# Loads of q and k for five of eight batches as casting transfers issued by GpSimd, and their turns split into 64 columns

## The chip, the cores and the metric

The kernel runs on one core of a Trainium2 chip. The metric is the device time of one launch in microseconds, lower is better. Matrix products and transposes run on TensorE (PE; PEld is its weight load), elementwise work on VectorE (DVE), ScalarE (ACT) and GpSimd (POOL). SyncE (SP) computes nothing here: it issues transfers between the chip's memory (HBM) and the on-chip buffer (SBUF). Products land in eight banks of a separate memory (PSUM).

## The reference

An attention in two parts, followed by a layer that mixes over tokens and channels. Cut to what is computed, with B = 8 batches, H = 8 heads, S = 576 positions, D = 64:

```python
q_d, k_d, v_d = means of q, k, v over groups of 4 positions          # 144 positions
out_d   = softmax(q_d k_d^T / 8) v_d, each row repeated 4 times
out_loc = softmax over |i - j| < 4 of (q k^T / 8), times v
x = (out_up + out_loc) as [B, S, H * D]                              # 576 x 512
theta = x @ w_theta
y = w_tok_r @ (x * cos(theta)) + w_tok_i @ (x * sin(theta))          # over positions
u = x + y
out = u + max(u @ w_ch, 0)
```

Inputs and output are float32; the kernel works in bfloat16 between.

## The kernel before

The kernel is a set of generators, one for each step of a batch: `load`, `cast`, `turns`, `turns_out`, `key_sums`, `query_sums`, the pooled attention, the local attention (`scores`, `masks`, `outputs`), then `phases`, `waves`, `products`, `mix`, `channels`, `store`. The string `ORDER`, written out by hand, says which step runs next, one letter each ("L" a load, "C" a cast, "A" a turn), with steps of several batches interleaved. `pin()` ties every instruction to the one before it on its engine, so each engine works in exactly this order, and an instruction that waits holds everything behind it on its engine. Waits between engines follow from the data. The string `BANKS` gives each product its bank, and `ENGINES` gives each copy its engine: the string `C` has one letter per cast (p GpSimd, a ScalarE, v VectorE).

How q and k of one batch come in:

- `load` (L213) issues, from SP's queue, eight transfers of 288 KB, two heads each (`k0` to `k3`, `q0` to `q3`, L223), into float32 staging tiles `st`, of which 15 rotate. A row holds 9 positions of 64 numbers (`WR` = 9), so a partition gets 2304 bytes in one piece. Five chunks of v follow, two transfers each (L220).
- `cast` (L226) copies each staging tile to bfloat16: `k_tm` and `q_tm`, two buffers each, laid out as [pair of transfers, position in the row, transfer, 64], so that the 128 columns of one position (two transfers of 64) lie next to each other. All copies share line 127.
- `turns` (L294) transposes on TensorE: for each of four groups (k of transfers 0 and 1, q of 0 and 1, k of 2 and 3, q of 2 and 3) nine transposes of 128 x 128 (L300) into two banks. Each needs both casts of its group.
- `turns_out` copies the result to `kT` and `qT`; from there go the sums over four positions (`key_sums` on VectorE, L317; `query_sums` on GpSimd, L334 and L335) and the local scores (L468).

GpSimd also does some of the casts of v and of the weights, the multiplies of `pooled_v_last` (L363, tile `vd`) and some of the copies `ut`. `pooled_v` (L348, L350) multiplies v on TensorE by 32-column matrices; L350 needs the fifth chunk of v. `weight_turns` (L276) transposes the token weights; its ninth group is made of transposes of 64 columns, two of them side by side onto the lower and the upper 64 partitions of a bank. The longest work on TensorE is `mix` (L654): nine products of 288 columns for each of 8 pieces of a batch. For batches 6 and 7, `x_turns_by_queue` borrows a `k_tm` buffer for transposes done by transfers (L628).

Of the kernel before, what the change touches and what calls it, by code (L numbers as in the profile page):

```python
# [9 lines left out]
BF16 = mybir.dt.bfloat16  # L10
# [4 lines left out]
P = 128  # L15
# [3 lines left out]
D = 64  # L19
# [15 lines left out]
WR = 9  # L35
# [2 lines left out]
HALF = 64  # L38

BY_QUEUE = [6, 7]  # L40

OC = 96

# [2 lines left out]
def kernel(  # L46
# [11 lines left out]
    nc = tc.nc  # L58
# [29 lines left out]
        C=(  # L88
            "vapaaaaavpvvappppppapppvpapppppppppppppvapvpappvappapppppppavpvapappaapppaaaaapppppaaaapapppappp"
            "appaavaa"  # L90
        ),
        a="avaavaaaavaaaaaaaaaaaaaaaaaaaaaa",
        c="aapapppappppppppappp",
        f="ppvpapap",
        q="vaaavvva",
# [8 lines left out]
    def rot(tag, shape, dt, n):  # L104
        k = turn[tag] = turn.get(tag, -1) + 1
        if (tag, k % n) not in made:
            made[tag, k % n] = const.tile(shape, dt, name=f"{tag}_{k % n}")
        return made[tag, k % n]
# [9 lines left out]
    def two(dt=FP32):  # L118
        i = int(next(banks)) // 2
        ap = space[:, 2 * i:2 * i + 2, :]  # L120
        return ap if dt == FP32 else ap.bitcast(dt)

    copies = dict(v=nc.vector.tensor_copy, a=nc.scalar.copy, p=nc.gpsimd.tensor_copy)
    engines = {s: iter(e) for s, e in ENGINES.items()}

    def copy(step, **operands):
        copies[next(engines[step])](**operands)  # L127
# [3 lines left out]
    def tile_of(name, shape, dt=BF16):  # L131
        return const.tile(shape, dt, name=name)

    ident = tile_of("ident", [P, P])
# [70 lines left out]
    staged, inputs = {}, {}  # L205

    def stage(key):
        t = staged[key] = rot("st", [P, S], FP32, 15)
        return t

    ITEMS = ["k0", "k1", "q0", "q1", "k2", "k3", "q2", "q3", "v0", "v1", "v2", "v3", "v4"]

    def load(b):  # L213
        for it in ITEMS:
            c = int(it[1])
            if it[0] == "v":
                t = stage((b, it))[:, 0:DM].rearrange("p (h d) -> p h d", d=D)
                for g in range(2):
                    lo = W0[2 * c + g]
                    nc.sync.dma_start(out=t[W * g:W * g + W], in_=v[b, :, lo:lo + W, :].rearrange("h p d -> p h d"))  # L220
            else:
                src = k if it[0] == "k" else q
                nc.sync.dma_start(out=stage((b, it)), in_=src[b, 2 * c:2 * c + 2].rearrange("h (p r) d -> (h p) (r d)", r=WR))  # L223
            yield

    def cast(b):  # L226
        k_tm = rot("k_tm", [P, 2, WR, 2, D], BF16, 2)
        q_tm = rot("q_tm", [P, 2, WR, 2, D], BF16, 2)
        v_w = v_ws[b % 2]
        inputs[b] = (q_tm, k_tm, v_w)  # L230
        for it in ITEMS:
            c = int(it[1])
            if it[0] == "v":
                copy("C", out=v_w[:, c, :, 0:D], in_=staged.pop((b, it))[:, 0:DM].rearrange("p (h d) -> p h d", d=D))
            else:
                dst = k_tm if it[0] == "k" else q_tm
                copy("C", out=dst[:, c // 2, :, c % 2, :], in_=staged.pop((b, it)).rearrange("p (r d) -> p r d", d=D))
            yield


# [53 lines left out]
    def turns(b):  # L294
        q_tm, k_tm, v_w = inputs[b]
        parts[b] = (rot("qT", [P, 4, S], BF16, 2), kTs[b % 2], rot("qdT", [P, 4, SD], BF16, 2), kds[b % 2])
        for i, what in TURNS:
            ps = held["turn", b, i, what] = two(BF16).rearrange("p k e -> p (k e)")
            for r in range(WR):
                nc.tensor.transpose(out=ps[:, P * r:P * r + P], in_=(k_tm if what == "k" else q_tm)[:, i, r, :, :], identity=ident)  # L300
            yield

    def turns_out(b):
# [318 lines left out]
    xms = {}  # L622

    def x_turns_by_queue(b):
        spare = rot("k_tm", [P, 2, WR, 2, D], BF16, 2).rearrange("p i r c d -> p (i r c d)")
        xm = xms[b] = spare[:, 0:4 * DM].rearrange("p (c n) -> p c n", c=4)
        for dc in range(4):
            nc.sync.dma_start_transpose(out=xm[:, :, P * dc:P * dc + P], in_=xTs[b][:, dc, 0:512])  # L628
            yield

    def products(b):
        for c in range(4):
            x = xms[b][:, c, :] if b in BY_QUEUE else held.pop(("xt", b, c))
            nc.vector.tensor_tensor(  # L634
# [108 lines left out]
    def each(steps, n=B):  # L743
        for b in n if isinstance(n, list) else range(n):
            yield from steps(b)

    sequences = {
        "k": constants(), "1": table(AF.Sin), "2": table(AF.Exp),
        "L": each(load), "C": each(cast), "l": weight_loads(), "c": weight_casts(), "V": weight_turns(), "v": weight_turns_out(),
        "A": each(turns), "a": each(turns_out), "d": each(key_sums), "e": each(query_sums),  # L750
        "U": each(pooled_v), "u": each(pooled_v_out), "x": each(pooled_v_last),
        "P": each(pooled_scores), "p": each(pooled_exp), "N": each(pooled_out), "n": each(pooled_norm),
# [3 lines left out]
        "T": each(transposes), "t": each(transposes_out),  # L756
        "H": each(phases), "h": each(waves), "G": each(tail_phases), "g": each(tail_waves), "Z": each(tail_product), "z": each(tail_z),
        "X": each(x_turns, [b for b in range(B) if b not in BY_QUEUE]), "M": each(x_turns_by_queue, BY_QUEUE), "y": each(products),
        "J": each(mix), "j": each(mix_out),
        "R": each(residual), "f": each(tail_gather), "F": each(tail_residual, B // 2),  # L760
# [40 lines left out]
```

## Time and profile before

| | |
|---|---|
| time, median of 2 runs | 244.81 us (244.55 to 245.08) |
| profiled execution | 245.89 us, of which the span from the first to the last instruction is 244.2 us |
| TensorE busy | 214.8 us (88% of the span) |
| VectorE, ScalarE, GpSimd busy | 191.3, 164.9, 95.0 us |
| transfers | 50.91 MB, mean 208 GB/s; SP's queue 91.7% of 16 engines' span |
| `st` from k and q | 64 transfers of 288 KB, median 4.8 and 5.3 us from issue to landing |
| casts of `q_tm` and `k_tm` | 64, about 0.67 us each: 43 on GpSimd, 18 on ScalarE, 3 on VectorE |

Busy times are of one profiled execution, so sums from it are set against its own span; the median is of other runs. A busy TensorE includes the modelled ends of pipelined products: a product counts 286 ns (L654) while the next one starts 122 ns later. The share of the transfers is the time that packets took on 16 engines; it can pass 1 in a stretch, since packets overlap. In the views, a line of the timeline has the start, the length, the engine, the line of the kernel, the tiles (out<-in), the form and the count, and in brackets the idle time before it with what ended it.

### The profile page before, as it was taken

Reading aid. Unit: us, or ns where it says so; the run is one execution under the profiler, and the core shown is the slowest. Engines: PE = TensorE matmul, PEld = TensorE weight load, DVE = VectorE, ACT = ScalarE, POOL = GpSimd, SP = SyncE. Lnnn points to the kernel's source line nnn. Section 1 sums busy time; section 2 is a strip of 40 time slices with the busy share of each in tenths; the row PEclk is TensorE's granted clock in tenths of the full one; section 3 lists DMA queues with packets and bytes.
Section 4 is the critical chain, followed back from the end, with each engine's and each line's share of the span. In section 5 each row is a group of like instructions: output and inputs, shape, how many; then the busy total and the mean of one; then the engine's idle time right before and its main releaser. Section 6 shows DMA issues by size and latency. Waiting matters only on the chain.

```text
span 244.2 us, 8224 instructions
## 1 busy us (share of the span) xinstructions
PE 214.8 (88%) x3344; PEld 151.8 (62%) x3344; DVE 191.3 (78%) x393; ACT 164.9 (68%) x240; POOL 95.0 (39%) x170
## 2 busy tenths in 40 slices
PE   1466586998999999799999999999999999999990
PEld 1354453776678685487775786676676765667740
DVE  3596977797789879779799988897798978585453
ACT  3786497699799899798899859866677653420000
POOL 1785585776574594272056115923021000000000
PEclk9999997799999999999999999999999999999997
DMA  6999989989999999999899989997531586966577
GB/s 203 280 211 295 278 179 241 312 206 189 263 299 227 280 273 149 194 267 268 194 244 271 146 240 262 283 217 161 99 124 51 136 124 159 173 170 154 59 230 229
DMA packets 87671, 50.91 MB, mean 208 GB/s; under 512 B 72529, under 2 KB 72785, under 8 KB 87633
## 3 DMA queue, kind: packets, MB, share of 16 engines
q1 hardware_dynamic: 87632, 50.38, 91.7%
q8 instruction: 26, 0.43, 0.8%
q14 instruction: 13, 0.10, 0.2%
HBM read 34.11 MB, written 9.44 MB: 178 GB/s over the span
## 4 chain that ended last, share of the span: by engine, by line
PE 47%; DMA 22%; DVE 13%; SPq 7%; POOL 3%; issue 3%; ACT 3%; DVEq 0%; ACTq 0%; POOLq 0%
PE space L654 18%; DMA st<-in_v_dram 10%; PE space L567 7%; PE space L693 6%; DMA st<-in_q_dram 5%; SPq L220 4%; PE space L300 3%; DVE osb L706 2%; PE space L500 2%; DMA st<-in_moe_w_tok_i_dram 2%; PE space L540 2%; SPq L255 2%; DVE z L634 2%; DMA ur<-uT 1%; SPq L628 1%
## 5 line engine op out<-in xcount | busy, mean ns | idle before, releaser
L654 PE MATMUL space<-WT,z 128*128 128x288 bf16 x576 | 79.4, 286 | 0.8 <-DVE uT L663 0.4
L654 PEld LDWEIGHTS <-z 128*128 128x128 bf16 x576 | 54.0, 98 | 17.1 <-issue 1.3
L663 DVE TENSOR_TENSOR uT<-space,xT 128x288 bf16<-128x288 f32 x64 | 28.1, 449 | 11.5 <-PE space L654 9.6
L567 PE MATMUL space<-wth,xT 128*128 128x512 bf16 x128 | 33.8, 389 | 0.1
L693 PE MATMUL space<-wch,uT 128*128 128x512 bf16 (+1 forms) x132 | 31.9, 373 | 0.0
L706 DVE SCALAR_TENSOR_TENSOR osb<-space,ur 128x512 f32<-128x512 f32 (+1 forms) x33 | 21.7, 666 | 10.1 <-DMA ur<-uT 6.4
L574 ACT ACTIVATE cs<-space,pihc 128x512 bf16<-128x512 f32 x32 | 22.2, 693 | 7.9 <-issue 3.9
L520 DVE TENSOR_TENSOR tmp<-space,rl 128x512 bf16<-128x512 f32 x40 | 26.7, 679 | 0.5
L552 DVE TENSOR_TENSOR xT<-space,xdT 128x464 bf16<-128x464 f32 (+1 forms) x40 | 24.7, 627 | 1.7 <-PE space L540 1.4
L317 DVE TENSOR_REDUCE kd<-kT 128x290 bf16<-128x1160 bf16 x16 | 21.6, 1353 | 2.8 <-ACT kT L127 2.8
L480 ACT ACTIVATE pm<-space 128x1024 bf16<-128x1024 f32 (+1 forms) x24 | 20.6, 882 | 3.6 <-PE space L468 3.4
L334 POOL TENSOR_TENSOR two<-qT 128x576 f32<-128x576 bf16 x14 | 16.2, 1157 | 15.6 <-ACT qT L127 8.6
L127 POOL CAST q_tm<-st 128x576 bf16<-128x576 f32 x23 | 15.6, 685 | 15.6 <-DMA st<-in_q_dram 15.2
L127 POOL CAST k_tm<-st 128x576 bf16<-128x576 f32 x20 | 13.9, 700 | 18.8 <-DMA st<-in_k_dram 17.7
L127 POOL COPY ut<-uT 128x256 bf16<-128x256 bf16 x5 | 2.3, 451 | 44.5 <-DVE uT L663 44.5
L127 POOL CAST v_w<-st 128x512 bf16<-128x512 f32 x16 | 10.0, 634 | 23.9 <-DMA st<-in_v_dram 21.8
L575 ACT ACTIVATE cs<-space 128x512 bf16<-128x512 f32 x32 | 19.1, 598 | 0.0
L127 ACT COPY qT<-space 128x1152 bf16<-128x1152 bf16 x14 | 15.7, 1120 | 4.8 <-PE space L300 4.7
L693 PEld LDWEIGHTS <-uT 128*128 128x128 bf16 x132 | 12.1, 98 | 10.6 <-issue 0.3
L127 ACT COPY kT<-space 128x1152 bf16<-128x1152 bf16 x15 | 17.0, 1132 | 2.3 <-PE space L300 1.9
L567 PEld LDWEIGHTS <-xT 128*128 128x128 bf16 x128 | 11.5, 100 | 10.2 <-issue 0.8
L300 PE MATMUL space<-ident,k_tm 128*128 128x128 bf16 x144 | 12.1, 236 | 6.4 <-ACT k_tm L127 6.1
(95 smaller groups left out, 397.1 us busy)
## 6 DMA issues: line engine op xcount, KB each, us to landing
st<-in_v_dram SPq DMA_DIRECT2D x80, 128.0 KB, 5.1
st<-in_k_dram SPq DMA_DIRECT2D x32, 288.0 KB, 4.8
st<-in_q_dram SPq DMA_DIRECT2D x32, 288.0 KB, 5.3
out_dram<-osb SPq DMA_DIRECT2D x31, 256.0 KB, 3.3
st<-in_moe_w_tok_r_dram SPq DMA_DIRECT2D x6, 216.0 KB, 5.1
st<-in_moe_w_tok_i_dram SPq DMA_DIRECT2D x6, 216.0 KB, 4.8
out_dram<-osb SPq DMA_DIRECT2D x10, 128.0 KB, 2.5
st<-in_moe_w_theta_dram SPq DMA_DIRECT2D x4, 256.0 KB, 6.3
```

The source lines that it names most:

```text
L127: copies[next(engines[step])](**operands)
L300: nc.tensor.transpose(out=ps[:, P * r:P * r + P], in_=(k_tm if what == "k" else q_tm)[:, i, r, :, :], identity=ident)
L317: nc.vector.tensor_reduce(out=kd[:, hs, :, 0:PG].rearrange("p e g m -> p (e g) m"), axis=AX.X, op=ALU.add, in_=kT[:, hs, :].rearrange("p e ...
L480: nc.scalar.activation(out=pm.rearrange("p e c j w -> p e (c j w)"), in_=held.pop(("S", b, u))[:, :, 0:4 * W * n], func=AF.Exp, scale=SCL)
L520: nc.vector.tensor_tensor(out=tmp.rearrange("p g (j d) -> p g j d", d=D), in0=held.pop(("loc", b, c))[:, :, :, 0:D], in1=rls.pop((b, c)).u ...
L552: nc.vector.tensor_tensor(out=xT[:, :, CH * c:CH * c + cnt].rearrange("p e (m j) -> p e m j", j=4), in0=held.pop(("xT", b, c))[:, :, 0:cnt ...
L567: nc.tensor.matmul(out=th, lhsT=xT[:, dc, P * c:P * c + P], rhs=wth[:, dc, :], start=(dc == 0), stop=(dc == 3))
L574: nc.scalar.activation(out=cs[:, 0, :], in_=th, func=AF.Sin, bias=pihc, scale=1.0)
L654: nc.tensor.matmul(out=ps, lhsT=z[:, j, P * dc:P * dc + P], rhs=WT[:, j, 288 * hf:288 * hf + 288], start=(j == 0), stop=(j == 8))
L663: nc.vector.tensor_tensor(out=uT[:, dc, cols], in0=held.pop(("u", b, dc, hf)), in1=xT[:, dc, cols], op=ALU.add)
L693: nc.tensor.matmul(out=ps, lhsT=uT[:, dc, P * c:P * c + P], rhs=wch[:, dc, cols], start=(dc == 0), stop=(dc == 3))
L706: nc.vector.scalar_tensor_tensor(out=osb, in0=ps, scalar=0.0, in1=rest, op0=ALU.max, op1=ALU.add)
```

## The change

For batches 3 to 7 (`BY_GPSIMD`), `load` issues nothing for q and k any more: the step stays in the order as an empty one. Where the cast stood, GpSimd issues a transfer from HBM straight into the bfloat16 tile, and the transfer casts on the way. The letter of the cast in the string `C` is read and dropped, so all other copies keep their engines; transfers that take the place of casts on ScalarE and VectorE are issued by GpSimd too. v is loaded and cast as before, and batches 0 to 2 still load q and k through the staging tiles.

So that a transfer can write each row in one piece, the tiles `k_tm` and `q_tm` are laid out as [pair, transfer, position, 64], for all batches. The 128 columns of one position no longer lie next to each other, so every turn is made of 18 transposes of 64 columns, two for each position, onto the lower and the upper 64 partitions. `ORDER`, `BANKS` and `ENGINES` stay as they are.

```diff
+BY_GPSIMD = [3, 4, 5, 6, 7]
...
+    def pair(src, b, c):
+        return src[b, 2 * c:2 * c + 2].rearrange("h (p r) d -> (h p) (r d)", r=WR)
+
     def load(b):
...
                 src = k if it[0] == "k" else q
-                nc.sync.dma_start(out=stage((b, it)), in_=src[b, 2 * c:2 * c + 2].rearrange("h (p r) d -> (h p) (r d)", r=WR))
+                if b not in BY_GPSIMD:
+                    nc.sync.dma_start(out=stage((b, it)), in_=pair(src, b, c))
             yield
 
     def cast(b):
-        k_tm = rot("k_tm", [P, 2, WR, 2, D], BF16, 2)
-        q_tm = rot("q_tm", [P, 2, WR, 2, D], BF16, 2)
+        k_tm = rot("k_tm", [P, 2, 2, WR, D], BF16, 2)
+        q_tm = rot("q_tm", [P, 2, 2, WR, D], BF16, 2)
...
-                dst = k_tm if it[0] == "k" else q_tm
-                copy("C", out=dst[:, c // 2, :, c % 2, :], in_=staged.pop((b, it)).rearrange("p (r d) -> p r d", d=D))
+                dst = (k_tm if it[0] == "k" else q_tm)[:, c // 2, c % 2].rearrange("p r d -> p (r d)")
+                if b in BY_GPSIMD:
+                    next(engines["C"])
+                    nc.gpsimd.dma_start(out=dst, in_=pair(k if it[0] == "k" else q, b, c))
+                else:
+                    copy("C", out=dst, in_=staged.pop((b, it)))
             yield
...
             for r in range(WR):
-                nc.tensor.transpose(out=ps[:, P * r:P * r + P], in_=(k_tm if what == "k" else q_tm)[:, i, r, :, :], identity=ident)
+                for c in range(2):
+                    nc.tensor.transpose(out=ps[D * c:D * c + D, P * r:P * r + P], in_=(k_tm if what == "k" else q_tm)[:, i, c, r, :], identity=ident)
             yield
...
     def x_turns_by_queue(b):
-        spare = rot("k_tm", [P, 2, WR, 2, D], BF16, 2).rearrange("p i r c d -> p (i r c d)")
+        spare = rot("k_tm", [P, 2, 2, WR, D], BF16, 2).rearrange("p i c r d -> p (i c r d)")
```

## The prediction

> **What bounds the kernel now.** I read the slices first, then the busy time by stage, then the timelines of TensorE and GpSimd around the turns of batches 3 to 5, and last the rows of the transfers.
>
> Slices of the page (busy tenths, 6.1 us each):
>
> ```profile
> PE   1466586998999999799999999999999999999990
> PEclk9999997799999999999999999999999999999997
> DMA  6999989989999999999899989997531586966577
> ```
>
> Until about 61 us TensorE has holes while the transfers stand at 9: that part waits for loads, and none of it is touched except the turns of batches 0 to 2. From then on TensorE is full at full clock. The same by stage (columns: stretch, its us, busy us of PE, PEld, DVE, ACT, POOL, clock, DMA share, GB/s):
>
> ```profile
> 61.00:204.00 143.00, 140.13 (x2327) 99.75 (x2328) 123.30 (x249) 113.66 (x164) 55.19 (x79) 1.00 0.97 207
> ```
>
> So where batches 3 to 7 are turned, TensorE is idle for 2.87 us of 143. What adds TensorE work or makes it wait there is paid in full; relief elsewhere can bring little. GpSimd has room (55 of 143).
>
> **Turns by 64 columns.** TensorE's timeline (start, length, line, form, count):
>
> ```profile
> 62.53 0.55 PE L276 MATMUL space<-ident,uT 96*128 96x96 bf16 x9
> 62.92 1.27 PE L654 MATMUL space<-WT,z 128*128 128x288 bf16 x9
> 64.12 0.32 PE L276 MATMUL space<-ident,uT 96*64 96x96 bf16 x6
> 64.36 0.38 PE L382 MATMUL space<-qdT,kd 64*64 64x144 bf16 x12
> ...
> 72.61 0.67 PE L300 MATMUL space<-ident,k_tm 128*128 128x128 bf16 x9
> 73.11 1.27 PE L654 MATMUL space<-WT,z 128*128 128x288 bf16 x9
> 74.21 0.39 PE L619 MATMUL space<-ident,xT 128*128 128x128 bf16 x4
> ...
> 101.61 0.46 PE L348 MATMUL space<-v_w,pu 128*32 128x512 bf16 x4
> 103.31 0.24 PE L350 MATMUL space<-v_w,pu 128*32 128x128 bf16 x4 [1.24 <-POOL v_w L127]
> ...
> 130.37 0.40 PE L348 MATMUL space<-v_w,pu 128*32 128x512 bf16 x4
> 130.60 0.23 PE L350 MATMUL space<-v_w,pu 128*32 128x128 bf16 x4
> ```
>
> A turn of nine takes 0.50 us from its start to the next work (72.61 to 73.11). The kernel has the new form already: L276 with 64 columns, three pairs onto two halves of the bank. Nine of 128 columns take 0.39 us there (62.53 to 62.92), 43 ns each; three pairs one after the other, each pair at that price, would be 0.13, and the six take 0.24 (64.12 to 64.36). So the two of a pair run side by side, with 0.11 on top. Getting in costs as well: nine L654 take 1.10 us ahead of whole-array work (73.11 to 74.21) and 1.20 ahead of the 64-column form (62.92 to 64.12). Together 0.21 us a turn. Behind 61 us are 20 turns; two of them touch each other and one already stands beside 64x64 work: 20 x 0.21 - 0.3 = **3.9 us**. Bounds: 2.0 (entry alone, 20 x 0.10) to 14 (pairs one after the other, 20 x (0.21 + 0.50)); I take the same form's row. The 12 earlier turns add 2.5 us of work in the stretch that waits for loads; the chain passes through three (30.48, 46.98, 49.39), so 0.6 at most; I take **0.4**.
>
> **Casts and loads removed.** 40 casts of about 0.67 us go (27 on GpSimd, 11 on ScalarE, 2 on VectorE), and 40 issues from SP's queue, some 0.5 us each. SP's row of loads is in order, so the v loads of a batch stand up to 4 us behind eight q and k issues (61.83 to 66.0 for batch 3). They move forward. What that is worth: the L350 at 103.31 waits for v4 of batch 4. L348 to L350 takes 0.23 us undisturbed (130.37 to 130.60) and 1.70 here, with 0.4 more at the L468 behind and 0.2 at the same place of batch 3: **-2.1**, bounds 0 and -2.9 (all idle time). ScalarE's 11 casts are 7.4 us of an engine busy for 113.66 of 143; of TensorE's remaining 0.8 us idle I give it all: **-0.8**. VectorE's two and GpSimd's 27 are under TensorE's work, at nothing; if VectorE set the pace they would be 1.4.
>
> **Transfers added on GpSimd.** Each q or k transfer now starts where GpSimd stood to cast. Its buffer is free long before (last read by the turns of two batches earlier, over 10 us before), so this wait costs nothing, and GpSimd no longer waits for q and k either. But the landing, once 2 to 5 us ahead of the cast, now comes behind that place. GpSimd's timeline:
>
> ```profile
> 67.13 1.18 POOL L363 TENSOR_TENSOR vd<-last,own 128x256 bf16<-128x256 bf16 x2 [0.71 <-DVE last L127]
> 69.51 1.17 POOL L127 CAST k_tm<-st 128x576 bf16<-128x576 f32 x1 [0.59 <-DMA st<-in_k_dram]
> ...
> 76.91 1.15 POOL L334 TENSOR_TENSOR two<-qT 128x576 f32<-128x576 bf16 x1
> ...
> 81.46 0.88 POOL L127 CAST v_w<-st 128x512 bf16<-128x512 f32 x1 [1.49 <-PE space L468]
> ```
>
> No GpSimd transfer is in this trace. The nearest rows (us from issue to landing last):
>
> ```profile
> st<-in_k_dram SPq DMA_DIRECT2D x32, 288.0 KB, 4.8
> st<-in_v_dram SPq DMA_DIRECT2D x80, 128.0 KB, 5.1
> k_tm<-xT SPq DMA_TRANSPOSE x8, 2.6
> ```
>
> Issue on GpSimd: bounds 0.66 (a cast) and 1.2 (the longest cast); I take 1.0. Landing from the start of the issue: 2.6 (the transpose; the first load, with nothing ahead of it, took 2.9) to 5.1; I take 3.5, nearer the unqueued rows, since these transfers leave SP's line, in which k loads land 0.74 us apart.
>
> Batch 3: the first vd multiply ends at 67.74, then k0, k1, a vd multiply of 0.61, q0, q1, k2, k3, q2, q3. Starts: k1 68.74, q1 71.35, k3 73.35, q3 75.35. Landings: 72.2, 74.9, 76.9, 78.9. The turns now start at 72.61, 74.90, 75.41, 77.01: **1.8 us late** at the last. By the low ends 0; by the high ends q3 starts at 76.75, lands at 81.85: 4.8.
>
> Batch 4: GpSimd's v3 cast waits for TensorE (81.46), which is now 1.8 + 0.8 (four turns) later: 84.0 to 84.7. Then k0, k1 (start 85.7, lands 89.2), the two query sums 1.9, q0, q1 (start 89.6, lands 93.1). The turns are due at 86.23 + 2.6 = 88.8 (0.4 late), and 88.05 + 3.2 = 91.25: **2.25 us late** in all. k2 to q3 then land before their turns (k3 at 96.3 for 95.88 + 4.7). By the low ends 0.3, by the high ends 4.5. What queues behind these issues: query sums and vd multiplies of the same batch, which TensorE's pooled scores wait for; they move with the turns.
>
> Batch 5: GpSimd reaches k1 with the copy of ut at 103.2, moved by some 5 us; its landings are within the turns, which moved as well: 0 (high ends: 1.5). Batches 6 and 7: GpSimd is past batch 5's q3 by about 117 and its next k0 was cast at 124.9; their turns have 6 to 18 us behind most casts: 0.
>
> **Sum:** 3.9 + 0.4 + 1.8 + 2.25 - 2.1 - 0.8 = +5.5. The profiled execution took 245.89 us with a span of 244.2; the median of the runs is 244.81. The span would be 249.7, and against the median I forecast **250.3 us**.
>
> The Trainium skill, DMA: Bandwidth & Descriptors, section "Anatomy of one DMA — SWDGE (gpsimd) path", gives a GpSimd transfer 2.0 us plus its bytes at 436 GB/s, 2.7 us for these 288 KB. By that price (an estimate) batch 3 is 1.0 late and batch 4 1.55, and the sum is 248.8; no row here shows it.
>
> **Rivals.**
> *Landings in time.* Issue 0.66, landing 2.6: 0.3 late in all, 244.81 + 4.3 + 0.3 - 2.9 = 246.5. For it: a queue of their own and GpSimd at 39%. Against: transfers are at 97% of their time in this stretch.
>
> *Faster than before.* One mechanism: SP's row of loads is what makes TensorE wait; without q and k, v comes early everywhere and ScalarE is free. Laying each matmul's start against the usual spacing of its line (122 ns for L654, 216 for L567), the excess over 0.13 us adds up to 8.3 us between 61 and 220 us, more than the 2.87 shown idle, since modelled ends hide some. Freed in three quarters, with turns at their low bound: 244.81 + 2.0 - 6.2 = 240.6. It decides only if no landing is late. Against: most of that excess follows VectorE and ScalarE.
>
> *Issues stretched by VectorE.* Of 43 casts of q and k on GpSimd 40 took 657 to 668 ns; the three of 865 to 1168 each ran beside a mask (L488) on VectorE, like the 69.51 above. If each issue is stretched by the worst, 0.5 us, to 1.5: batch 3's q3 starts at 78.85 and lands at 82.35, 5.3 late; batch 4 3.75 more; 244.81 + 5.5 - 4.05 + 9.05 = 255.3. Against: 3 of 43. [...]
>
> *Not what it says:* pairs one after the other, so that the 64-column turns double: 250.3 + 10 = 260. L276 speaks against.
>
> **How the numbers follow.** Forecast 0.42 (its own range 247.5 to 253.5), landings in time 0.25, stretched issues 0.22, faster 0.08, serial pairs 0.03. Two per cent, about what a measurement of this kernel can tell from no change, is 239.9 and 249.7. Slower: over half of the forecast's 0.42, the 0.22 and the 0.03, some 0.52; faster 0.03, at the end of its case; same 0.45. The range leaves out the serial pairs and the ends of the outer cases: 244 to 257.
>
> **What would show it.** Right: L300 x18 taking some 0.7 us to the next work; GpSimd issue rows near 1.0 us, 40 of them; TensorE waiting for a transfer ahead of the turns of batches 3 and 4, about 4 us in all, none in 6 and 7; no wait at L350 of batch 4. Wrong: no idle time ahead of those turns (landings in time), issues well over 1.2 us or waits in batch 5 too, or TensorE's turns over 1 us.

## The result and the profile after

| | before | after |
|---|---|---|
| time, median of 2 runs | 244.81 us (244.55 to 245.08) | 251.88 us (251.81 to 251.96) |
| profiled execution, its span | 245.89 us, 244.2 us | 251.96 us, 250.3 us |

The ratio is 1.029, with a 95% interval of 1.024 to 1.034: slower, by 7.1 us against the median and by 6.1 us from span to span. (The profiled execution of before lay 1.1 us above its median, that of after 0.1 above its own.) The forecast was 250.3 us: 0.6 of the 1.6 us that it missed by are in its sum (+5.5 against +6.1 from span to span), the other 1.0 in where the two profiled executions lie to their medians. Runs of one kernel come in a faster and a slower state; every ratio here compares fast runs alone, while a median is over all runs.

The slices of the page after, 6.26 us each:

```profile
PE   1573988898978999998999999999999999999991
PEclk9999997999999999999999999999999999999998
DMA  6999979999799999799985997799824655665576
```

The clock is as full as before. The 7 of TensorE in slice 17 of before, where v of batch 4 was waited for, is gone. New from 61 us on are the 7 and the 8 in slices 12 and 13 (69 to 81 us), where batch 3 is turned, and an 8 in slice 19. By stage, with the columns as before; the last line is the kernel before in the same 16 us:

```profile
61.00:204.00 143.00, 138.51 (x2450) 96.03 (x2451) 118.06 (x238) 104.50 (x148) 58.34 (x92) 1.00 0.97 159
66.00:82.00 16.00, 13.15 (x205) 9.09 (x205) 10.33 (x22) 10.51 (x14) 9.10 (x15) 1.00 1.22 199
66.00:82.00 16.00, 15.74 (x280) 12.06 (x276) 14.04 (x31) 15.15 (x21) 8.85 (x13) 1.00 1.20 263
```

TensorE stands idle for 4.5 us of the 143 instead of 2.9, and 2.85 of these lie in the 16 us around the turns of batch 3. There it was idle for 0.26 us before. TensorE's timeline says on what; L311 is the turn, L665 `mix`, L359 and L361 are `pooled_v`:

```profile
72.89 0.24 PE L311 MATMUL space<-ident,k_tm 128*64 128x128 bf16 x1
74.55 0.69 PE L311 MATMUL space<-ident,k_tm 128*64 128x128 bf16 x17 [1.42 <-DMA k_tm<-in_k_dram]
75.18 1.28 PE L665 MATMUL space<-WT,z 128*128 128x288 bf16 x9
77.07 0.24 PE L311 MATMUL space<-ident,q_tm 128*64 128x128 bf16 x1
77.64 0.69 PE L311 MATMUL space<-ident,q_tm 128*64 128x128 bf16 x17 [0.32 <-DMA q_tm<-in_q_dram]
78.49 0.24 PE L311 MATMUL space<-ident,k_tm 128*64 128x128 bf16 x1 [0.16 <-DMA k_tm<-in_k_dram]
79.43 0.69 PE L311 MATMUL space<-ident,k_tm 128*64 128x128 bf16 x17 [0.69 <-DMA k_tm<-in_k_dram]
81.26 1.08 PE L311 MATMUL space<-ident,q_tm 128*64 128x128 bf16 x18
...
90.09 0.57 PE L551 MATMUL space<-ident,tmp 128*128 128x116 bf16 x8
90.59 0.69 PE L311 MATMUL space<-ident,k_tm 128*64 128x128 bf16 x18
91.22 1.28 PE L665 MATMUL space<-WT,z 128*128 128x288 bf16 x9
...
106.57 0.40 PE L359 MATMUL space<-v_w,pu 128*32 128x512 bf16 x4
106.79 0.23 PE L361 MATMUL space<-v_w,pu 128*32 128x128 bf16 x4
106.95 0.46 PE L479 MATMUL space<-qT,kT 64*64 64x64 bf16 x32
...
107.47 1.28 PE L665 MATMUL space<-WT,z 128*128 128x288 bf16 x9
```

In batch 3 the first transpose of a turn runs and the other 17 wait: its first transfer has landed and its second has not. From x1 to x17 takes 1.66 us where it takes 0.04 when nothing is waited for. Laid against undisturbed starts, the waits are 1.6 (k of transfers 0 and 1), 0.5 (q), 0.3 + 0.9 (k of 2 and 3) and 0.3 us (the last q): **3.7 us**. The brackets show less, since they count from the modelled end of the product before. In batch 4 (90.59) the 18 run in one piece, behind no wait. The wait of 1.5 us between `pooled_v`'s two products, at 103.31 before, is gone (106.57 to 106.79).

Work that starts after these waits stays late: the same products of TensorE start 0.2 us later than before at 70 us, 4.5 later at 80 us, 4.7 at 100, 3.4 at 110 (behind the place where v was waited for), 5.0 at 130, 5.9 at 150 and 6.4 at 180.

GpSimd's timeline (L245 is the issue of a transfer, L374 the `vd` multiply, L345 a query sum):

```profile
67.88 1.26 POOL L245 DMA_DIRECT2D k_tm<-in_k_dram  x2
69.15 0.63 POOL L374 TENSOR_TENSOR vd<-last,own 128x256 bf16<-128x256 bf16 x1
69.71 1.12 POOL L245 DMA_DIRECT2D q_tm<-in_q_dram  x2
70.82 1.08 POOL L245 DMA_DIRECT2D k_tm<-in_k_dram  x2
71.86 1.10 POOL L245 DMA_DIRECT2D q_tm<-in_q_dram  x2
...
79.68 1.14 POOL L345 TENSOR_TENSOR two<-qT 128x576 f32<-128x576 bf16 x1 [6.10 <-ACT qT L129]
```

Two issues take 1.1 us, so GpSimd is through at 72.96; by the forecast's 1.0 us an issue it would have been 76.35. The transfers are not. The page's rows of landings and of the two queues (the queue's packets, MB, share of 16 engines' span):

```profile
st<-in_v_dram SPq DMA_DIRECT2D x80, 128.0 KB, 6.2
k_tm<-in_k_dram POOLq DMA_DIRECT2D x20, 144.0 KB, 6.3
q_tm<-in_q_dram POOLq DMA_DIRECT2D x20, 144.0 KB, 6.9
...
q1 hardware_dynamic: 81872, 38.59, 73.8%
q0 software_dynamic: 5760, 5.90, 17.3%
```

One by one, batch 3's landings (worked out from the trace; the trace has none for k0):

```
transfer   issued   landed   us after issue
k1         68.60    74.51    5.9
q0         69.71    76.67    7.0
q1         70.30    77.60    7.3
k2         70.82    78.45    7.6
k3         71.34    79.39    8.0
q2         71.86    80.57    8.7
q3         72.38    81.60    9.2
```

Issues are 0.5 us apart within a group, landings about 0.9 from q0 on. A packet of this queue (2304 bytes read, 1152 written) has a median of 107 ns, and a transfer is 8 packets on each of 16 engines: 0.86 us. The trace's packets show the line itself. Taken in the order of their starts, k0's begin 1.6 us after its issue (69.5 us), q1's 4.5 (74.8) and q3's 6.1 (78.5). From 75 to 78.5 us this queue starts 141 packets a microsecond, where 16 engines at 107 ns each would do 150. So the transfers stand in a line of their own, while v's stand on the same engines (share 1.22).

### The profile page after: what moved, and what is told of

It reads as the page before. It is cut to its first block, busy times and chain, and to the rows that moved or that the text cites. A ratio compares the mean times of both kernels' runs of the same rounds, so it can differ in the third digit from the quotient of the medians.

```text
span 250.3 us, 8741 instructions
## 1 busy us (share of the span) xinstructions
PE 221.9 (89%) x3632; PEld 152.5 (61%) x3632; DVE 191.3 (76%) x391; ACT 159.3 (64%) x229; POOL 99.1 (40%) x183
## 4 chain that ended last, share of the span: by engine, by line
PE 56%; DMA 19%; SPq 10%; POOL 6%; DVE 5%; issue 2%; ACT 0%; DVEq 0%; POOLq 0%; ACTq 0%
PE space L665 22%; PE space L704 8%; PE space L578 7%; DMA st<-in_v_dram 6%; PE space L311 5%; SPq L225 4%; DMA q_tm<-in_q_dram 4%; DMA st<-in_moe_w_tok_i_dram 3%; PE space L551 2%; PE space L511 2%; DMA st<-in_q_dram 2%; SPq L639 2%; DMA out_dram<-osb 2%; PE space L479 2%; PE space L425 2%
## 5 line engine op out<-in xcount | busy, mean ns | idle before, releaser
L665 PE MATMUL space<-WT,z 128*128 128x288 bf16 x576 | 79.5, 286 | 1.0 <-DVE uT L674 0.6
L665 PEld LDWEIGHTS <-z 128*128 128x128 bf16 x576 | 53.6, 98 | 18.2 <-issue 1.6
L345 POOL TENSOR_TENSOR two<-qT 128x576 f32<-128x576 bf16 x14 | 16.1, 1147 | 39.0 <-ACT qT L129 18.7
L374 POOL TENSOR_TENSOR vd<-last,own 128x256 bf16<-128x256 bf16 x16 | 9.9, 633 | 28.6 <-ACT last L129 25.6
L311 PE MATMUL space<-ident,k_tm 128*64 128x128 bf16 x288 | 14.0, 242 | 8.0 <-DVE pihc L165 4.2
L311 PEld LDWEIGHTS <-k_tm 128*64 128x64 bf16 x288 | 10.5, 122 | 12.1 <-DVE pihc L165 4.2
L645 DVE TENSOR_TENSOR z<-space,cs 128x1024 bf16<-128x1024 bf16 x24 | 16.1, 678 | 0.7 <-ACT cs L586 0.5
```

Source lines behind the costliest of these rows:

```text
L311: nc.tensor.transpose(out=ps[D * c:D * c + D, P * r:P * r + P], in_=(k_tm if what == "k" else q_tm)[:, i, c, r, :], identity=ident)
L665: nc.tensor.matmul(out=ps, lhsT=z[:, j, P * dc:P * dc + P], rhs=WT[:, j, 288 * hf:288 * hf + 288], start=(j == 0), stop=(j == 8))
```

## The experiments

Each edit is against the changed kernel unless said otherwise. "Delay" is the start of the same instruction less its start in the kernel before, each from the start of its span. Each trace is one execution: at 65 us, ahead of all turns of batch 3, the delay lies between -1.4 and +1.0 us in these kernels, so what counts is how it changes within one trace.

**Turns alone.** q and k of all batches by SP and through casts; layout and split turns of the change.

```diff
-BY_GPSIMD = [3, 4, 5, 6, 7]
+BY_GPSIMD = []
```

> The new layout and the turns by 64 columns for all batches, every q and k load and cast as before (no transfer on GpSimd). Theory: the turns cost 0.23 us each wherever TensorE is full; 20 of them behind 61 us are 4.6, the earlier 12 nearly nothing: 249.0 to 250.0, with a delay against before that grows by about 0.9 us per batch and has no jump. Rival: the turns hide in TensorE's waits for v of batch 4 and the like and the loss of the change is all waiting for transfers: 245 to 246.5.

Measured: 247.78 us, ratio 1.011 (1.006 to 1.015). That lies between the two expectations. The delay grows from -0.6 us in batch 2 to +2.9 in batch 7, with no jump up; it falls by 0.7 where v of batch 4 is waited for. So the turns cost some 3.5 us on the path, where 20 times 0.23 would be 4.6: the rest falls into waits that TensorE has anyway. The splitting is 1.1 of the 2.9 per cent by the ratios and 3.5 of 6.1 us by the delays, so between two and three fifths; the rest comes with the transfers.

**The first batch that GpSimd loads.** Is it batch 3's place that is bad, or is the first batch always late?

```diff
-BY_GPSIMD = [3, 4, 5, 6, 7]
+BY_GPSIMD = [4, 5, 6, 7]
```

> Batch 3 loads and casts q and k as before; GpSimd issues them for batches 4 to 7 only. Theory: the first batch that is loaded this way pays for eight transfers in one line (the last lands 9 us after its issue), and its lateness then covers the next ones; so TensorE's wait of 3.7 us ahead of the turns of batch 3 goes and one of 2 to 3.5 us ahead of those of batch 4 appears: 250 to 251.5. Rival: the wait belongs to the place of batch 3 (v loads crowd it): nothing appears at batch 4, 247.5 to 248.5.

Measured: 252.28 us, ratio 1.025 (1.014 to 1.036). The waits of batch 3 are gone, and ahead of the turns of batch 4, where the changed kernel has none, there is this:

```profile
87.19 0.24 PE L311 MATMUL space<-ident,k_tm 128*64 128x128 bf16 x1 [0.17 <-DMA k_tm<-in_k_dram]
88.50 0.69 PE L311 MATMUL space<-ident,k_tm 128*64 128x128 bf16 x17 [1.06 <-DMA k_tm<-in_k_dram]
90.90 0.24 PE L311 MATMUL space<-ident,q_tm 128*64 128x128 bf16 x1 [0.51 <-DMA q_tm<-in_q_dram]
92.38 0.69 PE L311 MATMUL space<-ident,q_tm 128*64 128x128 bf16 x17 [1.24 <-DMA q_tm<-in_q_dram]
```

By their starts, 3.5 us. The first batch pays, and its lateness is the cover of those behind it. The time missed the expectation by about a microsecond; 1.1 us is a hole in the middle of a turn at 169.70 whose end the profile puts to nothing ("issue").

**Issue where the load stood.** The transfers are issued by GpSimd's step in `load`, some steps earlier in the order, for all five batches.

```diff
     def load(b):
...
+                else:
+                    if b not in tms:
+                        tms[b] = tm_pair()
+                    nc.gpsimd.dma_start(out=tms[b][it[0]][:, c // 2, c % 2].rearrange("p r d -> p (r d)"), in_=pair(src, b, c))
...
     def cast(b):
...
                     next(engines["C"])
-                    nc.gpsimd.dma_start(out=dst, in_=pair(k if it[0] == "k" else q, b, c))
```

> GpSimd issues each q and k transfer of batches 3 to 7 at the place in the order where its load stood, not where its cast stood; all else as in the change. Theory: the wait ahead of the turns of batch 3 goes (3.7 us), the price of the turns stays: 247.5 to 249, TensorE waiting for no transfer ahead of L311-like lines of batches 3 to 7. Rival: GpSimd's own order holds these issues back as well (it waits for v casts ahead of them), or the earlier transfers delay the v loads: over 250.5.

Measured: 249.71 us, ratio 1.023 (1.016 to 1.031). No turn waits for a transfer any more, so lateness of the landings was the cause of those waits. The time is 0.7 us above the expectation, and its interval overlaps that of the change (1.024 to 1.034): it is the trace that shows the waits gone, not the time. But a new one stands in batch 5, on ScalarE and behind it on TensorE:

```profile
123.26 0.62 ACT L129 CAST v_w<-st 128x512 bf16<-128x512 f32 x1 [3.16 <-DMA st<-in_v_dram]
...
124.86 0.45 PE L520 MATMUL space<-v_w,pm 64*64 64x65 bf16 x32 [1.61 <-ACT pm L500]
127.34 0.37 PE L560 MATMUL space<-ident,tmp 128*128 128x116 bf16 x4 [0.84 <-ACT cs L595]
```

q and k of batch 6, in no hurry, are now issued at 107 to 114 us and land until 122, together with v of batch 5, which is in a hurry.

**Early for batches 3 to 5 only**, at the place of the cast for 6 and 7 (`EARLY = [3, 4, 5]`).

> GpSimd issues q and k of batches 3, 4 and 5 at the place of their load and of batches 6 and 7 at the place of their cast. Theory: no wait ahead of any turn, and the wait of 3.2 us for v of batch 5 on ScalarE that the early issue of batch 6 brought is gone too; what is left is the price of the turns less the gain at batch 4: 246 to 248. Rival: v of batch 5 waits all the same, since batch 5's own early transfers crowd it: 249 to 250.

Measured: 248.67 us, ratio 1.016 (1.010 to 1.023). Waits for transfers ahead of turns and the one for v of batch 5 are both gone. A hole of 1.1 us like that at 169.70 stands in a turn at 168.26, and the time is 0.7 us above the expectation.

**Half of each row.** Only 288 of the 576 numbers per row are loaded; the rest of the tile keeps what it held.

```diff
-                    nc.gpsimd.dma_start(out=dst, in_=pair(k if it[0] == "k" else q, b, c))
+                    nc.gpsimd.dma_start(out=dst[:, 0:288], in_=pair(k if it[0] == "k" else q, b, c)[:, 0:288])
```

> As the change, but each of GpSimd's transfers loads only the first 288 of a row's 576 numbers (the other half of the tile keeps what an earlier batch left there): half the bytes, as many pieces and issues. Theory: the line is paced by the bytes that a piece reads, so pieces take some 55 to 65 ns in place of 107, eight land at the pace of the issues, the last 5 us after its issue in place of 9.2, and TensorE waits under 1 us ahead of the turns of batch 3: 247.5 to 249. Rival: a fixed latency of a GpSimd transfer of 6 to 7 us or a price per piece: landings as in the change, 251 to 252.

Measured: 249.0 us (one run). Packets take 65 ns instead of 107, the issues the same 0.55 us. In batch 3, k0, with no other ahead of it, lands 5.8 us after its issue and k1 6.0, as with whole rows, but q3 6.4 instead of 9.2: the line hardly shows, the lead of about 6 us stays. Two waits of 1.7 us in all are left there, both in the first turn (and one of 0.4 in batch 4), where under 1 us was expected for batch 3:

```profile
72.82 0.24 PE L311 MATMUL space<-ident,k_tm 128*64 128x128 bf16 x1 [0.76 <-DMA k_tm<-in_k_dram]
73.75 0.69 PE L311 MATMUL space<-ident,k_tm 128*64 128x128 bf16 x17 [0.69 <-DMA k_tm<-in_k_dram]
...
76.27 0.69 PE L311 MATMUL space<-ident,q_tm 128*64 128x128 bf16 x18
```

So of the 3.7 us about 2 belong to the line and 1.7 to the lead, which a transfer has here before any other of its kind is ahead of it. What makes the lead 6 us in this place and 3.15 for a later transfer (below) is not shown; the engines' share differs little, 1.06 here from 67 to 73 us and 0.93 there.

**Places kept in SP's queue.** SP issues a transfer of 64 bytes a row where it issued q and k, so that v does not move forward. The rival was that v, moved forward, crowds GpSimd's transfers.

```diff
                 if b not in BY_GPSIMD:
                     nc.sync.dma_start(out=stage((b, it)), in_=pair(src, b, c))
+                else:
+                    nc.sync.dma_start(out=stage((b, it))[:, 0:16], in_=pair(src, b, c)[:, 0:16])
```

> As the change, but SP issues in the old places of the q and k loads of batches 3 to 7 a transfer of 64 bytes per row into the staging tile, which nobody reads: SP's row is as long as before, so the v loads of a batch stay where they were, with hardly any bytes more. Theory: what makes GpSimd's transfers late is their own line (eight at 0.9 us and more), so the wait ahead of the turns of batch 3 stays within 1 us of 3.7; and the early v was worth the 1.4 us at L361 of batch 4, which comes back: 252.5 to 254. Rival: the v loads that moved forward crowd the casting transfers; without them the wait at batch 3 falls under 2 us: 249 to 251.

Measured: 262.23 us, ratio 1.066 (1.058 to 1.075). v of batch 3 is issued at 65.5 to 78.8 us (66.3 to 76.8 in the kernel before, 62.0 to 73.2 in the changed one), and batch 3 still waits 3.0 us, so v's place is not what makes it late; the rival falls. The time is no price of that wait. The delay goes from 5 to 12 us between batches 3 and 5: TensorE waits 1.5 us for k of batch 5 (114.19), and more behind ScalarE, which waits 2.8 and 2.7 us for v of batch 5 (126.83, 132.03), and VectorE, which waits 2.3 us for `ur` (122.84). Besides, the granted clock is 0.50 from 78.7 to 82.1 us, behind the waits of batch 3. That small transfers cost this much was not expected by either theory. They also take staging tiles and SP's time again, and why this costs more than the whole loads did in the kernel before is left open.

**Whole turns, rows in pieces.** The tiles of before, turns of 128 columns, and transfers that write 128 bytes at a time.

```diff
-        k_tm = rot("k_tm", [P, 2, 2, WR, D], BF16, 2)
+        k_tm = rot("k_tm", [P, 2, WR, 2, D], BF16, 2)
...
-                    nc.gpsimd.dma_start(out=dst, in_=pair(k if it[0] == "k" else q, b, c))
+                    nc.gpsimd.dma_start(out=dst, in_=pair(k if it[0] == "k" else q, b, c).rearrange("p (r d) -> p r d", d=D))
```

> Layout and turns of 128 columns as before; GpSimd's transfers write each position of 64 numbers by itself (128 bytes) into that layout, nine pieces per row. Theory: the 4.6 us of the turns go, but a transfer has nine times the pieces: issue on GpSimd and time on the 16 engines rise (at the 18 ns of v's 256-byte packets a transfer would take 1.3 us of 16 engines against 0.85), so the waits for batches 3 and 4 grow: 249 to 256, with TensorE's waits ahead of the turns well over 3.7 us. Rival: pieces cost nothing that shows: 247 to 248.

Measured: 263.97 us (258.49 to 267.89 over four runs; the profile is of the longest), above the expectation even at its lowest. Packets are 1152 a transfer of 32 ns each, 2.3 us of 16 engines instead of 0.86, and an issue takes 1.0 us. Batch 3's transfers land 5.7 to 14.5 us after their issue:

```profile
74.55 0.66 PE L310 MATMUL space<-ident,k_tm 128*128 128x128 bf16 x9 [1.89 <-DMA k_tm<-in_k_dram]
80.19 0.69 PE L310 MATMUL space<-ident,q_tm 128*128 128x128 bf16 x9 [3.19 <-DMA q_tm<-in_q_dram]
85.10 1.12 PE L310 MATMUL space<-ident,k_tm 128*128 128x128 bf16 x9 [4.22 <-DMA k_tm<-in_k_dram]
```

Taken by their starts, the waits ahead of the four turns are some 11 us: nearly three times the packet time makes about three times the waiting, the line again. Not all of the lost time is waiting: behind the first waits the granted clock is 0.50 from 80.7 to 94.4 us. The run also says why the layout was changed.

**Plain transfers by GpSimd.** The kernel before, with batch 4's q and k issued by GpSimd at the place of the load, as float32 into the staging tiles, and cast as before.

```diff
+BY_GPSIMD = [4]
...
-                nc.sync.dma_start(out=stage((b, it)), in_=src[b, 2 * c:2 * c + 2].rearrange("h (p r) d -> (h p) (r d)", r=WR))
+                (nc.gpsimd if b in BY_GPSIMD else nc.sync).dma_start(out=stage((b, it)), in_=src[b, 2 * c:2 * c + 2].rearrange("h (p r) d -> (h p) (r d)", r=WR))
```

> The kernel before, but the eight q and k loads of batch 4 alone are issued by GpSimd at the place of their load, as plain float32 transfers into the staging tiles; casts, layout and turns as before. Theory: SP's row is free for v of batch 4, TensorE's 1.4 us at L350 of batch 4 go, and GpSimd pays eight issues of 0.55 us under TensorE's work: 0.5 to 1.5 us faster than before; pieces of 2304 bytes take about 93 ns on the engines, against 107 with the cast. Rival: the plain loads wait in GpSimd's order and come later than from SP, so casts of batch 4 are late: 0 to 3 us slower.

Measured: 254.47 us, ratio 1.045 (1.039 to 1.050), far more than either theory said. The casts of batch 4 stand on GpSimd behind the issues and wait for landings (4.8 us for k at 96.08), and they hold up all that comes behind them; TensorE waits 6.4 us at 102.49 for a weight's cast, and the granted clock is 0.50 from 100.0 to 106.8 us. So it is no test of the early v. On landings it says one thing: k2, issued at 90.15 with none of GpSimd's transfers ahead of it, landed after 5.8 us, so the lead of 6 us does not come from the cast on the way. Its packets took 213 ns for 4608 bytes, which is 107 for 2304, and SP's loads of q and k in the kernel before took 93 ns for packets of 2304 bytes: the cast on the way costs no more than these 14 ns a packet here.

**Whole turns where SP still loads.** Batches 3 to 5 by GpSimd, issued early, with split turns; all others as in the kernel before, turns included.

```diff
+                if b not in BY_GPSIMD:
+                    nc.tensor.transpose(out=ps[:, P * r:P * r + P], in_=tm[:, P * r:P * r + P], identity=ident)
+                    continue
                 for c in range(2):
```

> Batches 3 to 5 come in by GpSimd's transfers, issued where the load stands; batches 0 to 2, 6 and 7 keep the loads, casts and turns of the kernel before (nine turns of 128 columns), so only 12 of 32 turns are split. If what was left of the lag in the kernel with early issue for batches 3 to 5 was the price of the split turns (32 turns for about 3.5 us net), 20 whole turns give 2.2 us back: 246.5 us, with the delay of TensorE against the kernel before at 1.3 to 2 us from batch 5 on and not growing after it. If it was something else that comes with GpSimd's transfers (v and q in other order on the engines of the transfers), the time stays at 248 to 249.

Measured: 246.42 us beside 245.06 for the kernel before on that chip, ratio 1.008 (1.003 to 1.013). By the ratios that is 2 us less than the version with 32 split turns, as expected; from batch 4 on the delay stays about 1 us or less, where 1.3 to 2 was expected. The 2 us are not the turns' price by themselves: batches 6 and 7 are loaded by SP again too, and the hole of 1.1 us is in the other trace alone.

**The same for batch 4 alone** (`BY_GPSIMD = [4]`, `EARLY = [4]`).

> The same with batch 4 alone: four split turns (0.9 us) against the wait for v of batch 4 in the kernel before (1.7 us between the two products, 0.4 behind them). If both sizes hold and nothing else moves: 0.5 to 1 us below the kernel before, 243.8 to 244.4 us, the wait for v of batch 4 gone. If that gain was only TensorE's lateness hiding the wait, v still waits and the time is 245 to 246.

Measured: 244.78 us beside 245.06, ratio 1.002 (0.998 to 1.006): no difference, where 0.5 to 1 us was expected. The wait for v is gone (L375 and L377 are `pooled_v` there, L681 is `mix`):

```profile
102.92 0.40 PE L375 MATMUL space<-v_w,pu 128*32 128x512 bf16 x4
103.15 0.23 PE L377 MATMUL space<-v_w,pu 128*32 128x128 bf16 x4
...
103.83 1.28 PE L681 MATMUL space<-WT,z 128*128 128x288 bf16 x9
```

The delay falls from +1.3 us at the first of these products to -0.5 at the `mix`: 1.8 us. The +1.3 is from the four split turns and from a wait of 1.8 us for a cast of v of batch 2 at 67.20. That wait is ahead of the first transfer that GpSimd issues (73.82), so nothing shows that it comes from the change. The two take the gain back in this trace. No version here beats the kernel before by more than the measurement can tell.

## Why the prediction was right, step by step

| step | forecast, us | shown, us |
|---|---|---|
| 20 split turns | +3.9 | +4.6 (20 x 0.23); 3.5 alone on the path |
| earlier turns | +0.4 | +0.2 (delay at 70 us, within the scatter) |
| landings of batch 3 | +1.8 (0 to 4.8) | +3.7 |
| landings of batch 4 | +2.25 (0.3 to 4.5) | 0, covered by batch 3 |
| v of batch 4 | -2.1 | -2.0, but lateness alone would have covered it |
| ScalarE's casts | -0.8 | not shown; -0.4 is left over |
| span | +5.5 | +6.1 |

**Turns: right.** The kernel before had in this place:

```profile
85.83 0.57 PE L540 MATMUL space<-ident,tmp 128*128 128x116 bf16 x8
86.23 0.67 PE L300 MATMUL space<-ident,k_tm 128*128 128x128 bf16 x9
86.74 1.27 PE L654 MATMUL space<-WT,z 128*128 128x288 bf16 x9
```

90.59 to 91.22 is 0.63 us where nine took 0.50, and the eight L551 ahead of it take 0.50 instead of 0.40: 0.23 each, with 0.21 forecast from the kernel's own 64-column form. Pairs run side by side, and the rival of serial pairs is out.

**Issues: wrong, to the good.** 1.0 us with bounds of 0.66 and 1.2 was taken from casts; 40 issues took 0.53 to 0.73 with a median of 0.56, below the lower bound. The time of a cast said nothing of an issue here. That also ends the rival of stretched issues: none took 1.5 us, while VectorE was busy for 118 of 143 us. The Trainium skill (SBUF — State Buffer, section "SBUF: two separate sides") says that GpSimd cannot write a transfer's descriptors while VectorE runs an operation in a two-port mode; these issue times show no such stall.

**Landings: the step that failed.** The term "I take 3.5, nearer the unqueued rows, since these transfers leave SP's line" priced each transfer as if alone. Alone it was near: q2 of batch 6, issued at 140.06, 19 us after the one before it, landed after 3.15 us. The 2.7 us that follow from the Trainium skill's fit for one transfer (an estimate; DMA: Bandwidth & Descriptors, section "Anatomy of one DMA — SWDGE (gpsimd) path") lie close to that too. But where the engines of the transfers stand above 1 in share, the second landed 5.9 us after its issue, and eight in a row form a line of their own, 0.9 us each, which the last leaves after 9.2. Both lie above the bound of 5.1. Leaving SP's queue did not mean leaving the queue on the engines. (The prediction's second sum, by 2.7 us, has a slip: worked out as the first one, batch 4 comes to 1.45 us and the sum to 248.7.)

**Batch 4: covered.** The forecast moved batch 4's turns by batch 3's lateness of 1.8 us and found them 2.25 late still. They were moved by 4.5, and that was enough. Loading from batch 4 on shows the same sum from the other side: 3.5 us, in batch 4. Both batches together were priced at 4.05 and cost 3.7; that the size came out is luck in part: batch 3 was priced 1.9 us too low, batch 4 2.25 too high.

**v: the waits are gone, but not by v alone.** Behind the wait at 103.31 the kernel before had:

```profile
103.77 0.46 PE L468 MATMUL space<-qT,kT 64*64 64x64 bf16 x32 [0.22 <-ACT qT L127]
...
104.29 0.91 PE L654 MATMUL space<-WT,z 128*128 128x288 bf16 x6
```

From `pooled_v` of batch 4 to this `mix` it took 2.68 us (101.61 to 104.29); it now takes 0.90 (106.57 to 107.47). That is 1.5 us between the two products and 0.3 at the L468; the 0.2 of batch 3 are gone as well (87.72 to 87.95), so 2.0 of the 2.1 us came. But TensorE arrives 5.0 us later than before, and v of batch 4 had landed at 102.5 in the kernel before: this lateness would have covered the waits even with v in its old place. The prediction added the lateness and the relief as if each stood by itself. How much of it lateness gives shows with turns alone, where v is loaded as before:

```profile
103.15 0.40 PE L359 MATMUL space<-v_w,pu 128*32 128x512 bf16 x4
104.22 0.24 PE L361 MATMUL space<-v_w,pu 128*32 128x128 bf16 x4 [0.67 <-POOL v_w L129]
...
104.90 1.28 PE L665 MATMUL space<-WT,z 128*128 128x288 bf16 x9
```

TensorE comes 1.5 us late and leaves 0.6 late, a gain of 0.9. With batch 4 by GpSimd it comes 1.3 late and leaves 0.5 early, a gain of 1.8. So v's earlier place, with the casts of batch 4 that are gone, is worth some 0.8 us there, by one trace of each.

**ScalarE: not shown.** -0.4 is only what the other rows leave of 6.1, and it may be the turns falling into other waits, as they did alone. No run took these casts away by themselves.

The rival of landings in time (246.5) fell with the waits of batch 3. That of a faster kernel fell on its own condition, no late landing; and where that condition is met for batches 3 to 5 by early issues, the kernel is still slower (ratio 1.016), or with whole turns elsewhere 1.008.

## What to carry to other kernels

A transfer that takes the place of a cast has to be issued earlier than the cast stood, by its whole landing, and the landing to use is that of the last of its group, not that of a single one: packets a transfer times packet time over 16 engines gives the spacing of the line. The first batch pays and its lateness hides the rest, so two lateness terms in a row on one path are a maximum over moving due times more than a sum, and a wait that this lateness covers is not to be credited to another cause as well. Issue only what is due soon: the early loads of a batch that had time crowded out v of one that had none.

## What was unexpected of the hardware

- An issue on GpSimd took 0.53 to 0.73 us for 128 rows, with 2304 or 1152 bytes read per row alike, and 1.0 us for 1152 pieces.
- Pieces of 128 bytes written took 32 ns each, 1152 bytes in one piece 107: cut nine ways, the same bytes took 2.7 times as long.
- Behind long waits TensorE's granted clock fell to 0.50: for 3.4 us with places kept in SP's queue, 6.8 with plain transfers, 13.7 with rows in pieces; in the changed kernel, with waits of up to 1.6 us, it stayed full from 61 to 204 us. That the waits brought it is not shown.
- Eight transfers of 64 bytes a row from SP's queue for each of five batches made the changed kernel about 9 us slower (ratio 1.066 instead of 1.029), though they move next to nothing; why is open.
